# A new order of all steps, and fourteen zero products behind the first scores, in a banded-attention kernel with a gated projection

## The chip, the core and the metric

The kernel runs on one core of one Trainium2 chip. The time is the device time of one execution in microseconds (us); the median of several runs counts. A core has five engines that run side by side and wait for each other by semaphores: TensorE (PE, matrix products; PEld is its weight load), VectorE (DVE), ScalarE (ACT), GpSimd (POOL) and SyncE (SP, which here issues every transfer).

## What is computed

Eight batches of eight heads. 512 local tokens each see 32 global keys and the local keys within 32 positions; 32 global tokens see all 544 keys. The result, 8 times 544 rows of 512 numbers, goes through a gate of two products and two more products. All of it is float32.

```python
s_g = scale * q_g @ k_all.T;  out_g = softmax(s_g) @ v_all
s_l = concat(scale * q_l @ k_g.T, where(|i - j| <= 32, scale * q_l @ k_l.T, -1e9))
out_l = softmax(s_l) @ concat(v_g, v_l)
x = concat(out_g, out_l)            # 4352 rows of 512
h = ((x @ w1) * (x @ w2)) @ w3      # inner width 1024
return h @ w_out
```

## The kernel before

**Steps.** The work is cut into some 3700 steps, and each step is a small function that issues a few instructions. The names below are the tiles that the profile shows.

- `scores1` (L500) and `scores` (L515) write the scores `s` of a head or of a pair of heads. They are float32 products on 64 rows of the array, eight a pair. `minus_max` (L524, DVE) masks them, `exps` (L528, ACT) makes the exponentials in `P`.
- `transposes` (L556, L558) turn `P` on TensorE into `t` for the first 16 heads; later heads go through a transfer to memory and back (`own`). `values` (L653, L659) makes `av` from the turned weights in `PT` and `G`, `values_sum` adds the halves.
- `g_scores` (L701, L709) writes the scores `sg` of the global queries, `g_minus_max` (L728, DVE), `g_exps` (L735, ACT), `g_normalize` (L739 to L741, DVE), `g_transposes` (L747, L748, tile `tg`).
- `fold` (L944) multiplies w3 by w_out once, 64 products into the tiles `w`, from weights that come as 64-bit words and are put together by DVE and ACT (`unpack`, L864 to L868).
- `first` (L810 to L812) is the gate's product of one m and one half a or b: 12 products of 128x128 by 128x256 into `ap` or `bp`, three for each pair of heads since every operand is split in a high and a low part. There are 3264 such products. `gate_a`, `gate_b`, `gate_hi`, `gate_lo` turn a pair of results into the operands `gh` and `gl`.
- `second` (L842 to L844) is the last product, six of 128x128 by 128x512 into `acc`, 137 steps.

**What sets the order.** `list_schedule` places the steps on five engines: at each moment the engine that is free takes, of the steps whose inputs are there by the planner's own costs, the one with the smallest number in the table `DUE`. Every engine executes its instructions in the order in which they were placed, and so does SP with its transfers. After each placed step the kernel calls `idle_products` with what `IDLE` lists for that step: products on a tile of zeros that nobody reads. The planner doesn't know of these. Before, `IDLE` has seven products ahead of everything and two behind the first `sg`.

**What stands where.** The first 118 us hold `fold`, the first heads and the first global scores. Then `first` and `second` of one batch run beside the attention of the next; the last pair scores (`s31`) start at 693 us, and from about 735 us only `first` and `second` are left.

Of the kernel before, what the change touches and what calls it, by code (L numbers as in the profile page):

```python
# [30 lines left out]
def i(ap):  # L31
# [18 lines left out]
IDLE = {None: ((0, 128, 256), (0, 128, 256), (0, 128, 256), (0, 64, 256), (64, 128, 256), (0, 64, 256), (64, 128, 256),), ("sg", 0): ((0, 128, 256), (0, 128, 256),)}  # L50
# [258 lines left out]
def band_attention_glu_kernel(  # L309
# [1103 lines left out]
    with tc.manual_schedule(engines=None):  # L1413
        idle_products(IDLE[None])
        for _, n, e in list_schedule(steps, after, held):
# [6 lines left out]
            fn(*args)  # L1422
            idle_products(IDLE.get(k, ()))

# [60 lines left out]
```

## Time and profile before

| | |
|---|---|
| median of 3 runs | 841.6 us (841.11 to 842.97) |
| the profiled execution | 839.91 us |
| its span, first to last instruction | 838.1 us |
| busy: PE, DVE, ACT, POOL | 821.3, 525.6, 480.5, 327.4 us |
| granted TensorE clock, mean | 0.995 of 2.4 GHz |

The span is cut by the profiler's records; 1.8 us of the execution lie outside it. A matrix product starts while the one ahead of it still drains, so an engine that the page calls busy may run at different paces: the time from one start to the next is the pace, and the duration in a row is longer than that.

### The profile page before, as it was taken

To read this page: it belongs to the slowest core of one execution; us is meant where nothing else is said; L and a number is where in the kernel's file an instruction comes from. 1 tells how busy PE (TensorE), PEld (TensorE's weight loads), DVE (VectorE), ACT (ScalarE), POOL (GpSimd) and SP (SyncE) were. 2 spreads that over 40 slices of the span, in tenths; PEclk is the share of its full clock that TensorE was granted. 3 is DMA by queue.
4 is the path that set the end of the run, shared out by engine and by line. 5 is a ranking of instruction groups with operands and counts; after the bars stand their busy time and mean duration, and the time that the engine had idled before them with its cause. 6 is when DMAs were issued, how large, how long until landed. Compare 5 with 4: busy or idle time off the path is not lost.

```text
span 838.1 us, 17284 instructions
## 1 busy us (share of the span) xinstructions
PE 821.3 (98%) x5666; PEld 728.7 (87%) x5666; DVE 525.6 (63%) x1436; ACT 480.5 (57%) x1354; POOL 327.4 (39%) x429
## 2 busy tenths in 40 slices
PE   5999999999999999999999999999999999999998
PEld 4656679899999988998988999998999999999997
DVE  4767776756666756667767778876778755522111
ACT  3665767756666656566756576666665554422112
POOL 1112453623456554544534654554555433300000
PEclk8999999999999999999999999999999999999999
DMA  8786655434666667566666666766565544200000
GB/s 282 235 266 218 193 142 172 138 89 130 180 162 174 169 157 178 149 176 174 174 165 185 171 179 162 172 166 180 152 175 152 144 106 135 51 27 14 13 26 26
DMA packets 209842, 124.87 MB, mean 149 GB/s; under 512 B 138328, under 2 KB 171480, under 8 KB 209752
## 3 DMA queue, kind: packets, MB, share of 16 engines
q1 hardware_dynamic: 209752, 123.76, 54.0%
q8 instruction: 45, 0.74, 0.4%
q14 instruction: 45, 0.37, 0.2%
HBM read 89.52 MB, written 31.82 MB: 145 GB/s over the span
## 4 chain that ended last, share of the span: by engine, by line
PE 88%; DMA 4%; SPq 3%; DVE 2%; issue 1%; ACT 1%; POOL 0%; ACTq 0%; DVEq 0%; POOLq 0%
PE bp L810 7%; PE ap L810 7%; PE acc L842 7%; PE av L659 7%; PE bp L811 7%; PE bp L812 7%; PE acc L844 7%; PE ap L811 7%; PE acc L843 7%; PE ap L812 7%; PE w L944 7%; PE s L515 5%; PE av L653 3%; PE s L500 1%; DMA G<-gd 1%
## 5 line engine op out<-in xcount | busy, mean ns | idle before, releaser
L810 PE MATMUL ap<-x,w12h 128*128 128x256 f32 x544 | 154.0, 283 | 0.5 <-ACT as__4769 L816 0.5
L810 PE MATMUL bp<-x,w12h 128*128 128x256 f32 x544 | 153.8, 283 | 0.0
L811 PE MATMUL ap<-x,w12h 128*128 128x256 f32 x544 | 151.7, 279 | 0.0
L812 PE MATMUL ap<-x,w12l 128*128 128x256 f32 x544 | 151.7, 279 | 0.0
L811 PE MATMUL bp<-x,w12h 128*128 128x256 f32 x544 | 151.7, 279 | 0.0
L812 PE MATMUL bp<-x,w12l 128*128 128x256 f32 x544 | 151.6, 279 | 0.0
L528 ACT ACTIVATE P<-P,small 128x192 f32<-128x192 f32 (+1 forms) x256 | 121.1, 474 | 15.6 <-DVE small L524 14.9
L810 PEld LDWEIGHTS ap<-x,w12h 128*128 128x128 f32 x544 | 102.4, 188 | 4.8 <-issue 2.0
L810 PEld LDWEIGHTS bp<-x,w12h 128*128 128x128 f32 x544 | 102.3, 188 | 3.6 <-issue 1.6
L811 PEld LDWEIGHTS ap<-x,w12h 128*128 128x128 f32 x544 | 102.3, 188 | 1.5 <-issue 0.2
L811 PEld LDWEIGHTS bp<-x,w12h 128*128 128x128 f32 x544 | 102.3, 188 | 1.3
L812 PEld LDWEIGHTS bp<-x,w12l 128*128 128x128 f32 x544 | 102.9, 189 | 0.0
L812 PEld LDWEIGHTS ap<-x,w12l 128*128 128x128 f32 x544 | 102.9, 189 | 0.0
L524 DVE CUSTOM_DVE_ANT_0 P<-s,cs 128x256 f32<-128x256 f32 (+1 forms) x256 | 85.0, 385 | 4.2 <-PE s L515 2.7
L673 DVE TENSOR_TENSOR u<-av,cb 64x352 f32<-64x352 f32 x96 | 49.2, 520 | 46.3 <-ACT cb L441 45.1
L441 ACT COPY cb<-av 64x352 f32<-64x352 f32 x77 | 34.4, 447 | 59.0 <-PE av L659 51.7
L444 POOL TENSOR_TENSOR PT<-own,PT 128x512 fp32r<-128x512 f32 x36 | 48.1, 1337 | 32.1 <-ACT PT L441 23.1
L944 PE MATMUL w<-wo,w3f 128*128 128x512 f32 x128 | 59.7, 598 | 0.5 <-DVE w3f L868 0.5
L659 PE MATMUL av<-PT,vs 128*128 128x192 f32 (+3 forms) x384 | 52.8, 264 | 0.4 <-DMA PT<-TT 0.4
L515 PE MATMUL s<-kq,qp 64*128 64x192 f32 (+1 forms) x448 | 50.0, 362 | 0.0
L528 ACT ACTIVATION_READ_ACCUMULATOR P<-P,small 128x1 f32 x256 | 48.1, 188 | 0.0
L515 PEld LDWEIGHTS s<-kq,qp 64*128 64x128 f32 x448 | 39.2, 186 | 8.8 <-issue 2.2
(804 smaller groups left out, 1883.9 us busy)
## 6 DMA issues: line engine op xcount, KB each, us to landing
raw_w<-in_w_t_dram SPq DMA_DIRECT2D x24, 512.0 KB, 4.7
od<-tw SPq DMA_DIRECT2D x48, 256.0 KB, 2.5
own<-od SPq DMA_DIRECT2D x192, 64.0 KB, 2.5
kq<-in_kd_t_dram SPq DMA_DIRECT2D x32, 304.0 KB, 3.4
kpr<-in_kp_t_dram SPq DMA_DIRECT2D x32, 272.0 KB, 3.8
out_dram<-o_None SPq DMA_DIRECT2D x33, 256.0 KB, 2.8
qp<-in_q_t_dram SPq DMA_DIRECT2D x32, 256.0 KB, 3.4
R<-rd SPq DMA_DIRECT2D x64, 128.0 KB, 3.5
```

Of the source, the lines that this page charges most:

```text
L515: nc.tensor.matmul(st[:, x, c : c + w], q[r, 128 * e : 128 * e + 128], k[r, o : o + w], start=(e % 2 == 0), stop=True, skip_group_check=True)
L524: nc.vector.tensor_tensor_reduce(blk(n, e), s, masks[e], -0.125, 3.0e38, ALU.add, ALU.min, T["mn", n][:, e : e + 1])
L528: nc.scalar.activation(blk(n, e), blk(n, e), AF.Exp, bias=T["mn", n][:, e : e + 1], scale=-1.0, accum_out=T["sm", n // 2][:, n % 2, e : e ...
L659: nc.tensor.matmul(av[0:r, o : o + 32 * (s1 - s0)], v[:, 0:r], PT[:, s0:s1, y, j], start=False, stop=(j % 2 == 1 and (plain or y == 1)), s ...
L673: nc.vector.tensor_add(T["u", n // 2][r : r + 64, x], T.pop(("av", n, x))[r : r + 64, 0:352], T["cb", n][r : r + 64, x])
L810: nc.tensor.matmul(d, wh[:, k, c, :], x[:, 0, 0:w], start=(k == m % 2 == 0), stop=False, skip_group_check=True)
L811: nc.tensor.matmul(d, wh[:, k, c, :], x[:, 1, 0:w], start=False, stop=False, skip_group_check=True)
L812: nc.tensor.matmul(d, wl[:, k, c, :], x[:, 0, 0:w], start=False, stop=(k == 3), skip_group_check=True)
L842: nc.tensor.matmul(a, gh[:, m % 2, sl], wh[:, c], start=(m == 0), stop=False, **part)
L843: nc.tensor.matmul(a, gh[:, m % 2, sl], wl[:, c], start=False, stop=False, **part)
L844: nc.tensor.matmul(a, gl[:, m % 2, sl], wh[:, c], start=False, stop=(m in (5, 7)), **part)
L944: nc.tensor.matmul(T["w34", t], T["w3f", t, j // 4][:, j % 4], T["wo"][:, j], start=(j == 0), stop=(j == 7))
```

## The change

`DUE`, the table of one number a step, is replaced, and `IDLE` gets an entry: fourteen products on zeros behind step `("s", 0)`, the scores of head 0.

```diff
-IDLE = {None: (...), ("sg", 0): ((0, 128, 256), (0, 128, 256),)}
+IDLE = {None: (...), ("s", 0): ((0, 128, 256),) * 14, ("sg", 0): ((0, 128, 256), (0, 128, 256),)}
...
 DUE = tuple(int(x) / 100 for x in """
-    127000 102500 146000 347000 352500 321500 661500 103500 94000 191000 74500 1861000 161000 220000 490000 1831500 243500 18500 668000 298500 323500 996500 35000 491500
...
```

The matrix products are the same ones, 5233 before and 5247 after with the fourteen. Which step follows which on TensorE is different. Counted over the program, of the pair scores `s` 18 stood behind a step of `first` and 9 behind one of `second`; now it is 4 and 23. Of the values `av` of heads 16 to 63, 39 stood behind `first` and 15 behind `second`; now 14 and 34. Of the later global scores `sg`, 11 stood behind `first` and 7 behind `second`; now 23 and 1; 4 had a `second` behind them, now none. `first` and `second` follow each other 135 times before and 141 times after.

**Place 1, the start, TensorE.** Here are its first steps, before and after. `idle` are the zero products.

```order
L500 MATMUL s_142<-kq_114,qp_116 128x192
L500 MATMUL s_142<-kq_114,qp_116 128x256 x2
L500 MATMUL s_142<-kq_114,qp_116 128x192
L701 MATMUL sg_176<-kpr_137,QG_112 128x272 x2
L388 MATMUL idle_102<-vgs 128x256 x2
L701 MATMUL sg_191<-kpr_128,QG_112 128x272 x2
L944 MATMUL w_0_197<-wo,w3f_0_165 128x512
L556 MATMUL t_205<-cs,P_79 128x128 x4
L558 MATMUL t_205<-cs,P_79 128x128 x3
L944 MATMUL w_1_219<-wo,w3f_0_213 128x512
L747 MATMUL tg_228<-cs,Pg_187 128x128 x4
L748 MATMUL tg_228<-cs,Pg_187 128x128
```

```order
L500 MATMUL s_150<-kq_121,qp_116 128x192
L500 MATMUL s_150<-kq_121,qp_116 128x256 x2
L500 MATMUL s_150<-kq_121,qp_116 128x192
L388 MATMUL idle_102<-vgs 128x256 x14
L701 MATMUL sg_177<-kpr_114,QG_112 128x272 x2
L388 MATMUL idle_102<-vgs 128x256 x2
L701 MATMUL sg_192<-kpr_133,QG_112 128x272 x2
L556 MATMUL t_205<-cs,P_79 128x128 x4
L558 MATMUL t_205<-cs,P_79 128x128 x3
L747 MATMUL tg_226<-cs,Pg_189 128x128 x4
L748 MATMUL tg_226<-cs,Pg_189 128x128
L944 MATMUL w_0_241<-wo,w3f_0_214 128x512
```

Fourteen products came between `s` and the first `sg`. Two products `w` stood ahead of `tg`, on either side of `t`; now the first `w` stands behind `tg`. Both lists go on with the scores of the next head (`s1` in the text) and its values. Further on, the turned weights of head 1 (the second `t`) had scores and a `w` behind them and now have the values `av` of the same head behind them at once.

**Place 1, the start, VectorE.** The masks of head 0 (L524), the global scores (L728) and the weights (L864, L868), before and after.

```order
L524 ISA P_79,small<-s_142,cs 128x192
L524 ISA small 128x1
L524 ISA P_79,small<-s_142,cs 128x256
L524 ISA small 128x1
L524 ISA P_79,small<-s_142,cs 128x256
L524 ISA small 128x1
L524 ISA P_79,small<-s_142,cs 128x192
L524 ISA small 128x1
L864 TENSOR_SCALAR raw_w12s_1_135<-raw_w12s_1_135 128x256
L868 SCALAR_TENSOR_TENSOR raw_w12s_1_135<-raw_w12s_1_135 128x256
L728 ISA Pg_187,small<-sg_176,cs 64x544
L728 ISA small 64x1
```

```order
L524 ISA P_79,small<-s_150,cs 128x192
L524 ISA small 128x1
L864 TENSOR_SCALAR raw_w12s_1_129<-raw_w12s_1_129 128x256
L868 SCALAR_TENSOR_TENSOR raw_w12s_1_129<-raw_w12s_1_129 128x256
L728 ISA Pg_189,small<-sg_177,cs 64x544
L728 ISA small 64x1
L524 ISA P_79,small<-s_150,cs 128x256
L524 ISA small 128x1
L524 ISA P_79,small<-s_150,cs 128x256
L524 ISA small 128x1
L524 ISA P_79,small<-s_150,cs 128x192
L524 ISA small 128x1
```

Before, all four masks of head 0 stood ahead of the first L728; now three of the four stand behind it. Beyond these rows, the first merged `wo` (L868) stood ahead of the second L728 and now stands behind L741. On SP the first transfers were `kq`, `qp`, a block of weights, `QG`; they are now `kpr`, `qp`, `cs`, `kq`, a block of weights, `QG`, so that the scores of head 0, which need `kq` and `qp`, wait for the fourth transfer and no longer for the second, while the mask `cs` went from ninth to third and the `kpr` of the first `sg` from eleventh to first.

**Place 2, the last pair scores, TensorE.** The steps around `s31`, of before and after.

```order
L810 MATMUL bp6_0_6_8939<-x6_3_0_8376,w12h7_1059 128x256
L811 MATMUL bp6_0_6_8939<-x6_3_0_8376,w12h7_1059 128x256
L812 MATMUL bp6_0_6_8939<-x6_3_0_8376,w12l7_1060 128x256
L515 MATMUL s31_0_9049<-kq31_8421,qp31_8401 128x192 x2
L515 MATMUL s31_0_9049<-kq31_8421,qp31_8401 128x256 x2
L515 MATMUL s31_1_9054<-kq31_8421,qp31_8401 128x256 x2
L515 MATMUL s31_1_9054<-kq31_8421,qp31_8401 128x192 x2
L810 MATMUL bp6_1_0_9075<-x6_0_1_7460,w12h0_88 128x256
L811 MATMUL bp6_1_0_9075<-x6_0_1_7460,w12h0_88 128x256
```

```order
L842 MATMUL acc6_0_128_8700<-w34h5_882,gh__8969 128x512
L843 MATMUL acc6_0_128_8700<-w34l5_883,gh__8969 128x512
L844 MATMUL acc6_0_128_8700<-w34h5_882,gl__8994 128x512
L515 MATMUL s31_0_9055<-kq31_8448,qp31_8374 128x192 x2
L515 MATMUL s31_0_9055<-kq31_8448,qp31_8374 128x256 x2
L515 MATMUL s31_1_9060<-kq31_8448,qp31_8374 128x256 x2
L515 MATMUL s31_1_9060<-kq31_8448,qp31_8374 128x192 x2
L810 MATMUL ap6_1_0_8999<-x6_0_1_7478,w12h1_90 128x256
L811 MATMUL ap6_1_0_8999<-x6_0_1_7478,w12h1_90 128x256
```

`s31` stood between two steps of `first`; now a step of `second` stands ahead of it.

## Rows read from the trace of the kernel before

**Rows 1.** The page, busy time by engine: us, share of the span, instructions.

```profile
PE 821.3 (98%) x5666; PEld 728.7 (87%) x5666; DVE 525.6 (63%) x1436; ACT 480.5 (57%) x1354; POOL 327.4 (39%) x429
```

**Rows 2.** Timeline of PE: start us, duration us, engine, line, tiles, shape, count, idle.

```profile
255.27 0.28 PE L810 MATMUL ap<-x,w12h 128*128 128x256 f32 x1
...
259.91 0.28 PE L812 MATMUL ap<-x,w12l 128*128 128x256 f32 x1
...
738.74 0.28 PE L810 MATMUL ap<-x,w12h 128*128 128x256 f32 x1
...
744.27 0.28 PE L812 MATMUL ap<-x,w12l 128*128 128x256 f32 x1
```

**Rows 3.** Groups of PE by line in 255.2:260.2, 215:692, 695:832: count, busy us, mean ns.

```profile
L812 PE MATMUL bp<-x,w12l 128*128 128x256 f32 x8 | 2.2, 276 | 0.0
...
L812 PE MATMUL ap<-x,w12l 128*128 128x256 f32 x368 | 102.3, 278 | 0.0
...
L812 PE MATMUL bp<-x,w12l 128*128 128x256 f32 x128 | 36.0, 281 | 0.0
```

**Rows 4.** Timeline of PE around s31 and s11.

```profile
691.82 0.28 PE L810 MATMUL bp<-x,w12h 128*128 128x256 f32 x1
...
693.07 0.28 PE L812 MATMUL bp<-x,w12l 128*128 128x256 f32 x1
693.27 1.78 PE L515 MATMUL s<-kq,qp 64*128 64x192 f32 x16
694.99 0.38 PE L810 MATMUL bp<-x,w12h 128*128 128x256 f32 x1
...
249.99 1.78 PE L515 MATMUL s<-kq,qp 64*128 64x192 f32 x16
251.70 0.38 PE L810 MATMUL ap<-x,w12h 128*128 128x256 f32 x1
```

**Rows 5.** Timeline of PE in the first 31 us.

```profile
5.17 1.67 PE L500 MATMUL s<-kq,qp 64*128 64x192 f32 x8
13.56 2.15 PE L701 MATMUL sg<-kpr,QG 128*128 128x272 f32 x4 [6.72 <-issue]
15.51 1.91 PE L388 MATMUL idle<-vgs 128*128 128x256 f32 x4
17.21 1.50 PE L701 MATMUL sg<-kpr,QG 128*128 128x272 f32 x4
18.55 1.02 PE L944 MATMUL w<-wo,w3f 128*128 128x512 f32 x2
...
22.55 1.78 PE L500 MATMUL s<-kq,qp 64*128 64x192 f32 x8
...
30.76 0.49 PE L558 MATMUL t<-cs,P 128*128 128x128 f32 x3
```

**Rows 6.** Busy us of PE, PEld, DVE, ACT, POOL (count), PEclk, DMA share, GB/s.

```profile
16.00:17.00 1.00, 1.00 (x4) 0.82 (x3) 0.90 (x4) 0.69 (x1) 0.00 (x0) 0.50 1.21 250
```

**Rows 7.** Timeline of ACT and DVE in the first 33 us.

```profile
5.46 0.44 ACT L866 ACTIVATE raw_w12s<-raw_w12s 128x256 f32<-128x256 f32 x1 [3.45 <-DMA raw_w12s<-in_w_t_dram]
...
11.40 0.36 DVE L524 CUSTOM_DVE_ANT_0 P<-s,cs 128x192 f32<-128x192 f32 x1
...
15.75 0.72 DVE L728 CUSTOM_DVE_ANT_1 Pg<-sg,cs 64x544 f32<-64x544 f32 x1 [1.64 <-PE sg L701]
...
19.51 0.75 ACT L735 ACTIVATE Pg<-Pg,small 128x544 f32<-128x544 f32 x1 [2.67 <-DVE small L728]
...
20.05 0.69 DVE L868 SCALAR_TENSOR_TENSOR w3f<-raw_w 128x512 int32<-128x512 int32 x1
...
21.24 0.50 DVE L741 TENSOR_SCALAR Pg<-Pg,small 128x544 f32<-128x544 f32 x1
...
32.37 0.69 DVE L441 COPY PT<-t 128x512 f32<-128x512 f32 x1 [1.79 <-ACT G L441]
```

**Rows 8.** Waits of PE: waited for, us in total, times, longest us.

```profile
PE av L653 <- DMA G<-gd: 3.3, 5, 1.3
```

More of the change, by code (lines that the diff above doesn't have):

```diff
@@ L47 @@
 )
-IDLE = {None: ((0, 128, 256), (0, 128, 256), (0, 128, 256), (0, 64, 256), (64, 128, 256), (0, 64, 256), (64, 128, 256),), ("sg", 0): ((0, 128, 256), (0, 128, 256),)}
+IDLE = {None: ((0, 128, 256), (0, 128, 256), (0, 128, 256), (0, 64, 256), (64, 128, 256), (0, 64, 256), (64, 128, 256),), ("s", 0): ((0, 128, 256),) * 14, ("sg", 0): ((0, 128, 256), (0, 128, 256),)}
 MARGIN, LATE, MAIN = 0, 0.0, 1e9
```

311 rows, old and new, of the table DUE are left out of this document.

## The prediction, made before the changed kernel ran

> **What bounds the kernel now.** I read the page first. TensorE is busy for 98% of the span [rows 1], and among its waits only one kind comes to more than a microsecond in the body of the program: `av` on the transfer of `G`, 3.3 us in five waits [rows 8]. The rest of its idle time lies in the first 31 us. An order can therefore gain in two ways: fewer gaps, or the same products at a closer pace. Since a busy TensorE may run at different paces, I then took the timeline and divided the time between two starts by the number of products. From 255.27 to 259.91 there are 41 steps in 4.64 us, 113.2 ns each; from 738.74 to 744.27 there are 47 in 5.53 us, 117.7 ns [rows 2]. It is the same instruction, 128x128 by 128x256, with no wait in either stretch. The duration in a group's row tells the two apart: the mean is 276 ns where all are fast and 281 where all are slow [rows 3]. So a mean says how many were slow: 278 in 215 to 692 is two fifths (278-276 over 281-276), and 281 in 695 to 832 is all of them. With 12 products in each of 272 steps there are 3264, of which about 2150 lie in the middle stretch and 744 in the last. Slow are .4 x 2150 = 860 and 744, and at 4.5 ns each (117.7-113.2) they cost 3.9 and 3.3 us.
>
> What changes the pace is seen at the scores. At 691.82 to 693.07 there are 11 steps in 1.25 us, 113.6 ns each: fast. Then `s31` comes between two steps of `first` [rows 4], and behind it everything to the end is slow [rows 3]. From 195 us on seven pair scores met a fast `first` and had `first` behind them; all seven left the slow pace (first at 231, last at 693). Behind a `second` eight were measurable, and all eight left the fast one; 249.99 is one [rows 4]. A global score behind `first` with `second` behind it turned fast into slow three times of three. The values `av` mostly leave the pace as it was (changed in 2 of 23). That is a correlation in one trace, without a cause that I can show.
>
> The start is bound otherwise. TensorE ends `s` at 6.84 and has nothing until `sg` at 13.56 [rows 5]; while it idles the granted clock falls to .5 of 2.4 GHz, the level of 1.2, where it stands from 11.2 to 18 us [rows 6]. Two zero products (four records) take 1.70 us there, from 15.51 to 17.21 [rows 5].
>
> **The change part by part: the order behind the start.** No product is added or taken away behind the start, so the sum of durations at one pace is the same. Pair scores behind `second` go from 9 to 23, those behind `first` from 18 to 4, and none of the global scores has a `second` behind it any more. If I walk the new order with the successions above, the fast pace is kept for most of the middle, about 12% slow in place of 40%, since what remains are the four `s` behind `first` and the doubtful `av`: 2150 x .28 x 4.5 = 2.7 us. The last `s31` now stands behind `second`, so the tail starts fast; `first` and `second` alone kept the pace there before. Taking a tenth as slow, it gains 744 x .9 x 4.5 = 3.0 us. Together 5.7; I take **-5.5**. The bounds are 0, if the succession is not the cause, and -7.2, if all of both stretches is fast.
>
> The Trainium skill, page "TensorE: Matmul & The Clock Gate", section "Wait — 56ns, not 53.3ns?", speaks against this gain: it gives one pace for back-to-back products at 2.4 GHz, the columns over the clock and about 2.5 ns more, 109 ns for 256 columns. By it an order couldn't change the pace, and the term would be 0. The trace doesn't agree: it has two paces, 113 and 118 ns, and no run here shows 109.
>
> Waits: TensorE's other waits in the body add to some 7.6 us with the 3.3 of [rows 8]. In the new order the distance from each `s` to its masks, from `av` to its transfer and from `first` to the gate is about as long, counted in products between; some are shorter, as the values directly behind `t` of head 1, which the start includes. I take 0, with 2.5 either way (a third of the waits).
>
> **The start.** I walk it with the durations of the rows. `s` needed the second transfer and now needs the fourth. The third had landed by 5.46, when ACT was released by it [rows 7]; by count the fourth is there at 5.46 x 4/3 = 7.3 at most, 5.5 at least, and I take 6.7, nearer the later end because `kpr` and `cs` are large tiles. `s` takes 1.7 [rows 5]: 8.4. The zero products at the full clock are half of 1.70 for two, .43 each; fourteen take 6.0, to 14.4. They fill the gap, so the clock should stay up: the first `sg` took 1.95 from start to start, the two products 1.70, part of the second `sg` was slow too, and half of that (some 2.3 us) is no longer lost. `sg` at full clock is 1.0 to 1.1, to 15.5. VectorE's mask of it (L728) starts .24 behind and takes .72 [rows 7]: 16.4. In front of the second `sg` there now stand three masks of head 0, at .36 [rows 7] and somewhat more: 17.4. The order shows that this `sg` waits for VectorE. It ends at 18.5, its L728 at 19.3. From the start of ACT's L735, 19.51, to the end of L741, 21.74, are 2.23 [rows 7]; so L741 ends at 21.6. `tg` and the merge of the first `wo`, moved behind L741 (.3 and .69 as in the L868 of 20.05 [rows 7]) come to 22.6, one `w` at .86 to 23.5. So `s1` starts at 23.5 in place of 22.55 [rows 5], .95 late, with one `w` fewer done, .86. Then `av` of head 1 stands directly behind its `t`: before, `t` ended at 31.25 [rows 5] and its copies at 33.06 [rows 7], with `s` and `w` in between to hide that; now some 1.5 of the 1.8 us are open. The sum is .95 + .86 + 1.5 = **+3.3**. The bounds are -2.3, the clock alone with everything else covered, and +6.0, the fourth transfer at 7.3 with the merges of `wo` and the copies each later by their own length. What hides the fourteen products is the wait for the transfers that ended at 13.56; since `kpr` now comes first, that cover may be gone, and then they cost TensorE itself their six us less the clock, which is in the walk.
>
> **Sum.** 839.91 - 5.5 + 3.3 + 0 = 837.7 for the profiled execution. The median lies 1.7 above that execution, so 837.7 + 1.7 = **839.4** against 841.6.
>
> **The rivals.**
> 1. *The start costs nothing, the pace comes.* If the walk's waits are hidden (s0 is there at 5.5, copies are fast), the start gives 0 to -2.3: 841.6 - 5.5 = 836.1 down to 833.8. For it: the clock loss is in the rows. Against it: three masks and the merge really moved in front of `sg` and `w`.
> 2. *The pace doesn't come, the start costs.* This is the slower side. The pace of a stretch would be set by something other than what stands ahead of `s`, for instance by the phase in which the products meet VectorE's and ACT's reads, and the new order would be slow about as often: 841.6 + 3.3 = 844.9. It is slower than before by over 1.7 us when the slow share of the middle and the tail together, now 1604 of 2894 or 55%, stays above 43%: the gain is then under 2894 x .12 x 4.5 = 1.6 of the start's 3.3. By the page's rule named above the order couldn't move the pace either, and the sum is this one. For it: 7 of 7 and 8 of 8 are one trace; against it: the split is clean.
> 3. *The clock falls all the same.* After the fourteen, TensorE waits for masks (16.6 to 17.4) and for `tg` (18.5 to 21.6). If the granted clock falls to .5 in there as at 11.2, then up to six us of products run at half pace, 2 to 3 us more: 839.4 + 2.5 = 841.9.
> 4. *Nothing of it moves the time*: the paces keep their shares and the start loses what the clock gains: 841.6.
>
> **How the numbers follow.** The forecast 839.4 (837 to 842, the waits' 2.5 either way) has 45%; rival 1 18%, rival 2 17%, rival 3 10%, rival 4 10%. A measurement can tell about 0.2%, 1.7 us, from no change: faster is below 839.9, slower above 843.3. The forecast lies half a microsecond below that bound, so of its 45% I give 27 to faster and 18 to same; rival 1 is faster, rival 2 slower but for 1, rivals 3 and 4 together same with 13, faster with 3, slower with 4. That gives faster .48, same .32, slower .20. The range for 8 in 10 reaches from rival 1's middle, 834.5, to rival 2's 845.0. Both signs hold chances; the likeliest case alone is 837 to 842.
>
> **What would show it.** Pace: the means of L812 go from 278 to about 277 in the middle and from 281 to 276 or 277 in the tail, and `s31` has 113 ns behind it as ahead of it. If the tail is at 281, the succession isn't the cause. Start: granted clock 1.0 from the first `s` to the second, `s1` near 23.5, an idle of 1.5 ahead of the `av` behind the second `t`. If `s1` is at 22 or below, rival 1 holds; a clock of .5 between 18 and 22 is rival 3. Waits: `av` on the transfer of `G` between 1 and 6 us in all; above that, the new order has shortened a distance that I took as equal.

## The result and the profile after

The changed kernel took 851.76 us in the median of six runs (847.19 to 853.75), the kernel before 841.49 (841.11 to 843.04): a ratio of 1.0099 with a 95% interval of 1.0080 to 1.0118. It is slower, outside the range of the prediction, and on the side that had a chance of 0.20. Two of the six runs are at 847.2 and four between 851 and 854; the trace is of a short one, 847.22 us with a span of 845.4, 7.3 more than before. On another chip, beside the experiments, it took 847.12 against 838.79, 8.3 us more. The experiments are read against the runs of before on their own chip.

The page's busy time and the groups of L812 (engine, tiles, count, busy us, mean ns), in 215:692 and 695:832, answer to [rows 1] and [rows 3]:

```profile
PE 825.8 (98%) x5694; PEld 727.3 (86%) x5694; DVE 530.5 (63%) x1435; ACT 478.0 (57%) x1352; POOL 326.9 (39%) x432
```

```profile
L812 PE MATMUL ap<-x,w12l 128*128 128x256 f32 x360 | 100.4, 279 | 0.0
L812 PE MATMUL bp<-x,w12l 128*128 128x256 f32 x350 | 97.1, 278 | 0.0
...
L812 PE MATMUL ap<-x,w12l 128*128 128x256 f32 x128 | 35.4, 277 | 0.0
L812 PE MATMUL bp<-x,w12l 128*128 128x256 f32 x127 | 35.2, 277 | 0.0
```

The tail is fast now, 277 in place of 281. The timeline of TensorE around `s31` shows it as [rows 4] does for before (start us, duration us, line, tiles, count):

```profile
700.83 0.40 PE L844 MATMUL acc<-w34h,gl__8994 128*128 128x512 f32 x1
701.16 1.78 PE L515 MATMUL s<-kq,qp 64*128 64x192 f32 x16
...
704.36 0.28 PE L810 MATMUL bp<-x,w12h 128*128 128x256 f32 x1
...
705.60 0.28 PE L812 MATMUL bp<-x,w12l 128*128 128x256 f32 x1
```

From 704.36 to 705.60 are 11 steps in 1.24 us, 113 ns each, behind `s31`. In the middle the mean did not fall; the stretch at half clock shown below holds it up, and without that stretch, in `after_no_zeros`, it is 277. The start, to be read beside [rows 5], and the granted clock there, beside [rows 6] (the third number from the end is the clock):

```profile
1.19 4.29 PE L388 MATMUL idle<-vgs 128*128 128x256 f32 x14 [1.19 <-DVE vgs L385]
6.94 2.20 PE L500 MATMUL s<-kq,qp 64*128 64x192 f32 x8 [1.46 <-DMA kq<-in_kd_t_dram]
9.07 7.50 PE L388 MATMUL idle<-vgs 128*128 128x256 f32 x28
16.40 1.08 PE L701 MATMUL sg<-kpr,QG 128*128 128x272 f32 x4
...
22.73 0.63 PE L747 MATMUL tg<-cs,Pg 128*128 128x128 f32 x4 [1.87 <-DVE Pg L741]
...
24.50 1.78 PE L500 MATMUL s<-kq,qp 64*128 64x192 f32 x8
...
32.53 0.75 PE L653 MATMUL av<-G,PT 128*128 128x288 f32 x2 [2.11 <-ACT G L441]
```

```profile
8.00:11.00 3.00, 3.00 (x9) 2.11 (x8) 1.43 (x5) 1.08 (x4) 0.00 (x0) 0.52 0.94 293
11.00:14.00 3.00, 3.00 (x14) 2.63 (x13) 0.00 (x0) 0.00 (x0) 0.00 (x0) 0.92 1.10 345
```

The zeros stand from 9.07 to 16.40, 7.3 us, with the clock at half until a little past 11 us, and `s1` starts at 24.50. The first step of `first` starts at 125.0 us, at 118.8 before.

TensorE's waits (waited for: us in total, times, longest), which answer to [rows 8], and the clock behind the longest one of the middle:

```profile
PE av L653 <- DMA G<-gd: 5.8, 5, 1.8
...
PE bp L810 <- DVE g__5252 L820: 1.2, 1, 1.2
```

```profile
450.73 0.37 PE L653 MATMUL av<-G,vgs 128*128 128x288 f32 x1 [1.83 <-DMA G<-gd]
```

```profile
452.00:454.00 2.00, 2.00 (x11) 2.00 (x11) 0.63 (x2) 1.74 (x6) 0.35 (x2) 0.50 0.71 179
```

Behind 1.83 us of waiting the clock falls to .5, and 15 products of `first` take 217 ns each: another 1.6 us. So the change did what it says, the tail got the pace that was forecast, and yet more was lost elsewhere. To see where, I priced each step of TensorE at the lowest tenth of the times that its kind took from start to start in the traces of before, after and fourteen of the experiments below, took zeros as nothing, and subtracted the sum from the time elapsed. What is left is the time lost in gaps, slow paces and zeros, by stretch:

```
us lost                 to 118  118-215  215-480  480-700  700-end   sum
before                    19.3      5.4     12.6      5.8      3.1  46.2
before_s31                19.5      5.7     10.7      5.3      0.7  41.9
after                     25.3      4.5     17.4      4.8      1.5  53.5
after_no_zeros            20.5      3.8     17.0      4.5      1.2  47.0
before_no_g               19.3      5.8      7.7      7.2      3.1  43.1
after_no_zeros_no_g       21.9      4.0      8.3      5.1      1.4  40.7
```

The first and the third row differ by 7.3, the difference of the spans: 6.0 of it at the start, 4.8 between 215 and 480 us, and 3.5 gained in the rest. The split is good to a microsecond or two: each row is one execution, `before_s31` stands 4.3 below `before` where their spans differ by 4.9, and it lost 1.9 less between 215 and 480 us although nothing was changed there.

### The profile page after: what moved, and what is told of

Same layout as the page of the kernel before. It is cut to its first block, busy times and chain, and to the rows that moved or that the text cites. A ratio compares the mean times of both kernels' runs of the same rounds, so it can differ in the third digit from the quotient of the medians.

```text
span 845.4 us, 17383 instructions
## 1 busy us (share of the span) xinstructions
PE 825.8 (98%) x5694; PEld 727.3 (86%) x5694; DVE 530.5 (63%) x1435; ACT 478.0 (57%) x1352; POOL 326.9 (39%) x432
## 4 chain that ended last, share of the span: by engine, by line
PE 83%; DMA 5%; SPq 4%; DVE 2%; ACT 2%; issue 2%; POOL 1%; ACTq 0%; POOLq 0%; DVEq 0%
PE av L659 7%; PE ap L810 7%; PE w L944 7%; PE acc L844 6%; PE acc L842 6%; PE ap L811 6%; PE ap L812 6%; PE acc L843 6%; PE bp L810 6%; PE bp L811 6%; PE bp L812 6%; PE s L515 4%; PE av L653 3%; PE s L500 2%; DMA G<-gd 2%
## 5 line engine op out<-in xcount | busy, mean ns | idle before, releaser
L812 PE MATMUL ap<-x,w12l 128*128 128x256 f32 x544 | 151.4, 278 | 0.0
L812 PE MATMUL bp<-x,w12l 128*128 128x256 f32 x544 | 150.9, 277 | 0.0
L812 PEld LDWEIGHTS ap<-x,w12l 128*128 128x128 f32 x544 | 102.9, 189 | 0.0
L812 PEld LDWEIGHTS bp<-x,w12l 128*128 128x128 f32 x544 | 102.5, 188 | 0.0
L524 DVE CUSTOM_DVE_ANT_0 P<-s,cs 128x256 f32<-128x256 f32 (+1 forms) x256 | 85.3, 384 | 7.5 <-PE s L500 3.6
L444 POOL TENSOR_TENSOR PT<-TGr,PT 128x128 fp32r<-128x128 f32 x38 | 18.4, 485 | 87.3 <-ACT PT L441 66.9
```

What stands on the lines that cost most here:

```text
L524: nc.vector.tensor_tensor_reduce(blk(n, e), s, masks[e], -0.125, 3.0e38, ALU.add, ALU.min, T["mn", n][:, e : e + 1])
L812: nc.tensor.matmul(d, wl[:, k, c, :], x[:, 0, 0:w], start=False, stop=(k == 3), skip_group_check=True)
```

## The experiments

**The same kernel again: `after_again`.**

> The changed kernel once more, unchanged, to see what its times of 847.2 (two of six) and 851.5 to 853.7 (four of six) consist of. If the extra 4.6 us come from the granted clock falling to .5 behind waits of TensorE (as behind the wait of 1.83 us at 448.9 us in the trace of after, where it stood at .5 for some 3 us), a trace of a longer execution shows more such stretches, each worth 1.5 to 2.3 us, at the waits of the start or of av on G. If they come from the pace of the products, its mean of L812 between 695 and 832 us goes back from 277 to 281 ns. If from the transfers, the waits of av on G are longer in sum than the 5.8 us seen.

Measured: 847.12 us (840.95 to 849.90), ratio 1.0087 (1.0057 to 1.0117). The profiled execution, 849.21, has its first step of `first` at 128.2, 3.2 later than the shorter execution of the first trace, and the middle and the tail as there. At its start the clock stays at .5 for longer, and falls once more behind the wait for `tg`:

```profile
11.00:14.00 3.00, 3.00 (x9) 2.37 (x8) 0.09 (x1) 0.00 (x0) 0.00 (x0) 0.50 1.04 334
...
26.00:29.00 3.00, 3.00 (x8) 1.46 (x7) 2.20 (x5) 1.14 (x4) 0.00 (x0) 0.65 0.67 193
```

The zeros took 8.4 us here. The first theory holds for these two traces: between one execution and the next the clock at the start makes some 3 us. In the middle each of the two traces has one fall of the clock, at 452 and 455 us. A still longer execution, 855.61 us, was traced in `after_s31`; it has its fall at 280 us instead. What makes the rest of the spread of 9 us was not seen.

**The zeros alone: `after_no_zeros` and `before_zeros`.** One entry of `IDLE` is taken out of the new order, or put into the old one:

```diff
-IDLE = {None: (...), ("s", 0): ((0, 128, 256),) * 14, ("sg", 0): ((0, 128, 256), (0, 128, 256),)}
+IDLE = {None: (...), ("sg", 0): ((0, 128, 256), (0, 128, 256),)}
```

> The new order without the fourteen zero products (the old IDLE table). Theory 1: in the new order nothing keeps the first sg waiting behind s, so the zeros are in the path: they stood from 9.07 to 16.40 us; without them the first sg starts at 9 to 10 us, at half the clock until about 13, s1 at some 19 in place of 24.50, and the time falls by 4 to 6 us, to about 842 for the short executions. Theory 2: the start is bound by the loads of weights and masks, which run on beside the zeros; then the first step of first still starts near 125 us and the time falls by less than 1.5 us. Theory 3: the clock that the zeros keep up is worth more than their length; then the time rises by 1 to 3 us.

> The old order with the fourteen zero products behind the first s. There the first sg waited until 13.56 us for its eleventh transfer, 6.72 us. Theory 1: the zeros fit into that gap (6.84 to 12.8 us at full clock, to 14.2 if they run at half the clock at first as in the trace of after, where they took 7.33 us); the granted clock then stays up from 11 to 18 us and the time falls by 1 to 2.3 us, to about 839.5 to 840.5. Theory 2: what the products gain is lost in waits on masks and exponentials behind them; the time stays within 0.7 us of 841.5.

Measured: the new order without zeros 843.05 us, ratio 1.0051 (1.0037 to 1.0065), so by the medians the zeros cost 4.1 us there, by the ratios 3.0, and the two intervals overlap a little; the traces are clearer. Nothing kept the first `sg` waiting once they were gone:

```profile
7.07 3.32 PE L500 MATMUL s<-kq,qp 64*128 64x192 f32 x8 [0.94 <-DMA kq<-in_kd_t_dram]
10.32 2.18 PE L701 MATMUL sg<-kpr,QG 128*128 128x272 f32 x4
...
19.51 1.78 PE L500 MATMUL s<-kq,qp 64*128 64x192 f32 x8
```

`s1` starts at 19.51 and `first` at 120.0, 5 us earlier. Theory 1 holds. The old order with the zeros took 837.48, ratio 0.9990 (0.9970 to 1.0009): its trace has the clock at 1.00 through the start, the zeros run from 7.45 to 13.76 and `sg` starts at 14.11, `first` at 117.2, 1.6 earlier than in the old trace. The median agrees in size (1.3), but the interval takes in no change: not settled.

```profile
5.84 1.67 PE L500 MATMUL s<-kq,qp 64*128 64x192 f32 x8
7.45 6.31 PE L388 MATMUL idle<-vgs 128*128 128x256 f32 x28
```

**The pace: `before_s31` and `after_s31`.** One step is moved on TensorE, by name, behind the planner: in the old order a step of `second` to directly ahead of `s31` (there `sp`, 31), in the new one a step of `first` (there with the longer code of the next experiment, which does the same).

```diff
+MOVED = ((('second', 12, 5, None), ('sp', 31)),)      # after_s31: (('first', 13, 1, 0), ('sp', 31))
...
-        for _, n, e in list_schedule(steps, after, held):
+        order = list_schedule(steps, after, held)
+        for a, b in MOVED:
+            name = [steps[n][0] for _, n, _ in order]
+            x = order.pop(name.index(a))
+            name.remove(a)
+            order.insert(name.index(b), x)
+        for _, n, e in order:
```

> The old order with one step moved on TensorE: the step of second that stood three steps of first ahead of the last pair scores s31 now stands directly ahead of them. Nothing else is moved. Theory 1 (what stands ahead of the scores sets the pace behind them): the last 744 products of first run at 113 and no longer at 118 ns, the mean of L812 between 695 and 832 us falls from 281 to 276 or 277, and the time falls by 3.0 to 3.3 us, to about 838.3. Theory 2 (the succession only went along with something else, such as the time at which the products meet the other engines): the mean stays at 281 and the time within 0.7 us of 841.5.

> The changed kernel with one step moved on TensorE: a step of first that stood directly behind the last pair scores s31 now stands ahead of them, so that s31 stands between two steps of first as in the kernel before. Theory 1 (what stands ahead sets the pace): the tail goes back to 118 ns, the mean of L812 between 705 and 830 us from 277 to 281, and the time rises by 3.0 to 3.3 us over the changed kernel, to a ratio of 1.0125. Theory 2: any move near s31 may turn the pace by chance; then the tail may stay at 277 and the ratio at 1.0087.

Measured: `before_s31` 835.43, ratio 0.9960 (0.9945 to 0.9976), 3.4 us less; `after_s31` 848.93, ratio 1.0117 (1.0085 to 1.0149), 1.8 us over `after_again`, which ran on another chip; the ratios are 0.0030 apart, 2.5 us. The groups of the gate's product in 705:830, first of `before_s31` (where the line is L815, three lines further down), then of `after_s31`:

```profile
L815 PE MATMUL bp<-x,w12l 128*128 128x256 f32 x114 | 31.5, 277 | 0.0
```

```profile
L812 PE MATMUL bp<-x,w12l 128*128 128x256 f32 x108 | 30.4, 281 | 0.0
```

Both ways one step decides the pace of all that follows. In the time lost from 700 us on, `after_s31` has 4.6 and the changed kernel 1.5, the 3.1 that were expected; the times alone, with intervals that overlap, would not show it. In the trace of `before_s31` the tail makes 2.4 of the 4.3 us that were won; the rest lies ahead of the move and is the difference between two executions.

**The pace in the middle: `before_scores`.** `MOVED` has seven pair scores and three global ones; a step takes along those that need it or that it needs (`out` and `store`, for instance).

```diff
+MOVED = (
+    (('second', 1, 7, None), ('sp', 10)), (('second', 4, 7, None), ('sp', 16)), (('second', 6, 7, None), ('sp', 20)),
...
+    (('first', 2, 4, 1), ('second', 2, 0, None)), (('first', 3, 0, 1), ('second', 2, 5, None)),
...
+)
```

> The old order with all seven pair scores that had turned the fast pace into the slow one put directly behind a step of second (s10, s16, s20, s21, s22, s27, s31; out and store move with the second where they depend on it), and at three global scores (sg11, sg12, sg29) the step of first that came second now ahead of the step of second. Theory 1 (what stands ahead of the scores sets the pace): nearly all steps of first from 215 us on run at 113 ns, the mean of L812 falls to 277 in the middle and in the tail, and the time falls by 5 to 6 us, 3.4 of it what s31 alone gave: ratio 0.993 to 0.994. Theory 2 (only the tail can be turned): ratio 0.996, as with s31 alone, and the middle stays at 278.

Measured: 837.62, ratio 0.9978 (0.9961 to 0.9994), no better than `s31` alone. L812 is 277 in the tail and 278 in 215:692, and the middle lost 12.3 us, like before. The numbers are those of theory 2, but its reason is not: the changed kernel turned the middle. Counted by step between 215 and 703 us, 68 of 204 were slow before, 57 of 204 here and 27 of 195 in the changed kernel: the moves turned few of the steps, since the pace fell into the slow one in other ways, behind `av` and `sg` above all, and what was won is not in the time. At the pair scores themselves the succession holds. I went through all 18 traces of this document from 195 us on (several have the same order again) and took every group of pair scores that has `first` directly behind it. Where a `second` stood ahead, that `first` was fast 267 times of 272; where a fast `first` stood ahead, it was slow 64 times of 64.

**The waits: `after_no_zeros_av` and `after_no_zeros_sp`.** The first moves steps of TensorE (`first` of m 0 for batch 2, for instance) ahead of the values that waited, the second moves transfers on SP:

```diff
+    (('first', 2, 0, 1), ('av', 17, 0)), (('first', 3, 1, 0), ('av', 21, 0)), ...      # _av
+    (('mi', 17), ('me', 17)), (('mi', 21), ('invo', 11)), ...                          # _sp
```

> The new order without the zeros, and with one or two steps of first (one of second too) moved from behind the values av of heads 17, 21, 25, 35, 37 and 39 to ahead of them: there TensorE waited for the transfer of G or PT, in the trace without the zeros some 1.9, 1.2, 2.3, 1.3, 3.3 and 1.0 us from the start of the step ahead to av, and at head 37 the granted clock fell behind the wait. Theory 1: the 4.3 us by which the order without zeros was slower than the kernel before are these waits and the clock behind them; the moved steps fill them, the waits of av on G fall from 6.0 to under 2 us, the stretch from 215 to 480 us gets 5 us shorter, and the time falls from 1.005 of the kernel before to 0.999 or below. Theory 2: the transfer of G is issued behind the end of the values of the head before, and SP, ACT or POOL move on with TensorE's delay; the waits stay or turn up at the gate, and the time stays within 0.002 of 1.005. Theory 3: what is lost lies in the start; the same numbers as theory 2, but with the waits gone.

> The new order without the zeros, TensorE's order untouched; only on SP the transfer of G from memory (L602) for the heads 17, 21, 25, 35, 37 and 39 is issued ahead of what stood between it and the values of the head before (the edges into PT, L591 and L592, and for some heads the loads of k and v or the sums). Theory 1 (SP's order makes TensorE wait for G): the waits of av on G fall from 6.0 to under 3 us and the time by 2 to 4 us, ratio 1.000 to 1.003. Theory 2 (the edges are wanted just as soon): the waits move to PT and the ratio stays within 0.0015 of 1.005.

Measured: 843.80, ratio 1.0050 (1.0033 to 1.0067), and 843.46, ratio 1.0066 (1.0039 to 1.0093): neither gained. The waits in 118:830, of `after_no_zeros`, of `_av` and of `_sp`:

```profile
PE av L653 <- DMA G<-gd: 6.0, 4, 3.0
```

```profile
PE bp L810 <- DVE g__3561 L820: 1.7, 1, 1.7
PE ap L810 <- ACT as__5768 L816: 1.6, 1, 1.6
PE av L653 <- DMA G<-gd: 1.3, 2, 0.9
PE bp L810 <- DVE g__2299 L820: 1.3, 1, 1.3
```

```profile
PE av L659 <- DMA PT<-TT: 2.3, 3, 1.1
PE acc L844 <- DVE gl__5186 L444: 1.8, 1, 1.8
```

The waits on `G` fell from 6.0 to 1.3 and 0.9 us, and others came up at the gate, or at the edges in `PT`: theory 2 in both, with `_sp` at the edge of its bound (1.0066 for 1.0065). The clock is not it either. The expectation has it fall at head 37, but that was the trace with the zeros; without them the products behind that wait, the longest of all, ran at full pace:

```profile
445.39 0.37 PE L653 MATMUL av<-G,vgs 128*128 128x288 f32 x1 [2.99 <-DMA G<-gd]
...
446.66 0.28 PE L811 MATMUL ap<-x,w12h 128*128 128x256 f32 x1
```

So these waits look like the places where a chain through other engines shows; filling one moved it.

**Less work for TensorE: `before_less` and `after_no_zeros_less`.** In `second`, for odd m of the batches 1 to 3, the product with `w34l` is left out:

```diff
-            nc.tensor.matmul(a, gh[:, m % 2, sl], wl[:, c], start=False, stop=False, **part)
+            if m % 2 == 0 or key[0] not in (1, 2, 3): nc.tensor.matmul(a, gh[:, m % 2, sl], wl[:, c], ...)
```

> The kernel before with less work for TensorE between some 240 and 490 us: in second, for the batches 1 to 3 and odd m, the product of gh with the low part of w3*w_out (L843) is left out, 6 x 4 x 2 products of 229 ns, 11.0 us. If TensorE sets the time of this stretch, the time falls by 9 to 11 us; if the transfers and the other engines set part of it, by less, since TensorE then waits for what it no longer covers. For the order of before, where TensorE waited for some 4 us in this stretch, both theories expect 7 to 10 us: ratio 0.988 to 0.992.

> The same products left out (L843 for batches 1 to 3 and odd m, 11.0 us) in the new order without the zeros, whose ratio with all products was 1.005. Theory 1 (in the new order a loop through SP, the transfers, VectorE and GpSimd sets the pace between 215 and 480 us, so that waits filled at one place turn up at another): the time falls by much less than before's, by 6 us or less, ratio 0.998 or above. Theory 2 (TensorE sets the time there too, and its waits are single accidents of the order): it falls by as much as before's, ratio 0.993 to 0.997.

Measured: 835.06, ratio 0.9947 (0.9928 to 0.9967), and 838.50, ratio 0.9993 (0.9970 to 1.0016): 4.4 us less than before (2.8 to 6.0 by the interval), where 7 to 10 were expected, and 4.9 less than 1.0051, which was measured on another chip. Of 11.0 us taken from TensorE four to five came back as time, in both orders. Executions differ: the one traced in `before_less` is the shortest of nine and has a span 8.1 us shorter than before. Theory 1 falls as I had put it, since the old order is no different; so does theory 2, that TensorE sets the time. In the new order the waits of `av` on `G` rose to 10.1 us:

```profile
PE av L653 <- DMA G<-gd: 10.1, 6, 2.8
```

Behind three of them, of 2.09, 2.51 and 2.84 us, the granted clock fell to .5, which the trace of `after_no_zeros` doesn't have:

```profile
224.00:227.40 3.40, 3.40 (x18) 3.40 (x17) 2.47 (x5) 2.55 (x7) 3.21 (x7) 0.50 0.19 54
...
445.80:449.20 3.40, 3.40 (x18) 3.40 (x18) 1.77 (x4) 2.74 (x8) 1.75 (x5) 0.51 0.84 203
```

The products of `first` in them start every 213 ns in place of 113, so these falls cost some 1.5 us each: in this execution a good part of what did not come back is the clock behind longer waits.

**The loop through memory: four kernels.** The edge weights of a head go from `TT` to memory (`gd`) and back into `G`, and from `TT` into `PT`, all issued by SP; a head's may land only when the values of the head before are done. The longest wait of the middle in the changed kernel shows the way of one head, on SP:

```profile
440.47 1.09 SPq L597 DMA_DIRECT2D gd<-TT  x2
...
444.15 0.64 SPq L591 DMA_DIRECT2D PT<-TT  x1
...
446.15 0.99 SPq L602 DMA_DIRECT2D G<-gd  x2
```

The second part of `gd` landed at 444.11 and the values of the head before were done by then, but SP was busy with other transfers until 446.15; `G` landed at 450.59, and `av` started at 450.73. These transfers are left out for heads 18 to 41:

```diff
             k = steps[n][0]
+            if k[0] in ('mo', 'mi') and 17 < k[1] < 42:      # _pt: ('mo', 'mi', 'me')
+                continue
```

> The kernel before, with the way of the edge weights through memory left out for heads 18 to 41 (some 237 to 490 us): the transfers of TT to gd (L597) and of gd to G (L602), 96 issues on SP; G keeps older numbers, all else is computed. Theory 1 (this way, SP's issues and the landing, is the loop that takes back what TensorE gains in the middle): TensorE's waits on G are gone, 3.3 us in the whole trace, and SP is freer; the time falls by 2 to 4 us, ratio 0.995 to 0.998. Theory 2 (the edges into PT or the gate take its place at once): ratio 0.998 or above.

> The new order without the zeros, with the same transfers (L597, L602, heads 18 to 41) left out. Theory 1 (in the new order this loop closes later, and that is its loss in the middle): the waits on G, 6.0 us, and the fall of the clock at head 37 go, and the time falls by 4 to 6 us to the time of before_no_g or below, ratio 0.998 to 1.000 from 1.005. Theory 2 (another loop takes over, as when the values were moved or SP's order was changed): ratio 1.003 or above.

> As before_no_g, and the transfers of the edges from TT into PT (L591, L592) left out too for heads 18 to 41. Theory 1: no more than before_no_g, within 0.001. Theory 2: now the waits are gone, ratio 0.995 to 0.998. If the gate's chain through ACT and VectorE bounds the stretch, neither brings more than 0.002.

> The new order without the zeros, the transfers into G and those of the edges into PT both left out for heads 18 to 41. Theory 1: as after_no_zeros_no_g, within 0.001. Theory 2, in the form that G and the edges come one behind the other on SP and only both together are the loop: ratio 0.997 to 1.000. Theory 3 (the loss lies with the gate's chain, L816 to L820, and the masks on ACT and VectorE): ratio 1.003 or above, with waits on these.

Measured, with the kernels above for comparison:

```
                               old order                   new order, no zeros
all work                       1                           1.0051 (1.0037 to 1.0065)
without gd and G               0.9961 (0.9946 to 0.9976)   0.9922 (0.9897 to 0.9947)
without the edges in PT too    0.9946 (0.9932 to 0.9960)   0.9920 (0.9904 to 0.9936)
```

The row of all work in the new order was measured on another chip than the four kernels. The old order gains 3.3 us, the new one 10.8, nearly twice what its waits on `G` came to, and more than the 4 to 6 that were expected; that the edges in `PT` bring anything more is not shown, since the intervals overlap. TensorE's waits on `G` in 118:830, 6.0 us with all transfers, are down to 1.4 in the new order:

```profile
PE av L653 <- DMA G<-gd: 1.4, 1, 1.4
```

The time lost in 215 to 480 falls from 12.6 to 7.7 and from 17.0 to 8.3, so that the 4.4 between the orders there shrink to 0.6. Theory 1 holds in this: the new order's loss in the middle goes with these transfers, which cost it 7.5 us more than the old order by the medians (some 5 to 10 by the intervals) and 3.8 by these traces. With them gone the new order is 3.3 us faster than the old one, the two intervals all but apart. That comes near what the tail's pace is worth in `before_s31`, but the traces do not put it there alone: they differ by 2.4, of which the tail makes 1.7, the stretch from 480 to 700 us 2.1 and that from 118 to 215 us 1.8, while the start loses 2.6 and the middle 0.6.

Two things stay open. Which moves of the new order make the transfers dearer was not found; SP's order of six transfers is not it. And a rival was not tested: leaving them out also takes 96 issues off SP, which issues everything in order. Added up from its rows, SP is issuing for 204 of the 265 us from 215 to 480 in the kernel before (77%), and for 156 without `gd` and `G`. Whether it is this one way through memory or SP's full queue as a whole, the runs do not say. SP's share alone doesn't make the loss: from 480 to 700 us it is 73% in the old order and 74% in the new one, and less time is lost there.

**A version that beats both: `before_best` and `before_s31_best`.** The old order, the zeros, `s31`, and a step of `first` ahead of the values of heads 25, 27 and 37; `before_best` has the other scores of `before_scores` too.

```diff
+MOVED = (
+    (('second', 12, 5, None), ('sp', 31)), (('first', 4, 0, 1), ('av', 25, 0)),
+    (('first', 4, 5, 1), ('av', 27, 0)), (('first', 7, 0, 1), ('av', 37, 0)),
+)
...
+IDLE = {None: (...), ("s", 0): ((0, 128, 256),) * 14, ("sg", 0): ((0, 128, 256), (0, 128, 256),)}
```

> The moves of before_scores, the fourteen zero products behind the first s in the old order, and one step of first moved ahead of the values av of heads 25, 27 and 37, where TensorE waited for G. Sum of the parts: 5 to 6 us of pace, 1 to 1.8 of the start, 2 of waits: 8 to 9 us, ratio 0.990. If the parts are in each other's way (the start's gain waited away later, since the loads don't come earlier), the ratio is that of before_scores within 0.001.

> The old order with only those changes that had a place of their own: s31 behind a step of second, the fourteen zeros behind the first s, and one step of first ahead of the values of heads 25, 27 and 37. If the six other moves of scores in before_best bring nothing, as the runs of before_s31 (0.996) and before_scores (0.998) suggest, the ratio is that of before_best, 0.9941, or lower: 0.992 to 0.994. If they bring their two to three us of pace, it is 0.996.

Measured: 834.24, ratio 0.9941 (0.9924 to 0.9957), and 833.37, ratio 0.9920 (0.9894 to 0.9946), 5.2 and 5.7 us less than before. Both beat both kernels; between them the intervals overlap. The first falls short of the 8 to 9 us of its sum, the second lies where it was expected. Their intervals overlap with that of `before_s31` (0.9945 to 0.9976) too, the second's by a hair, so what the zeros and the three moved steps add to `s31` is not shown.

## Why the prediction was wrong

- **What bounds the kernel: wrong, and the root of it.** "TensorE is busy for 98%" was taken to mean that a microsecond of TensorE is a microsecond of time. At 11.0 us less work it was two fifths of one between 240 and 490 us (a quarter to a half by the interval). A busy share of 98% and a way through other engines that is just hidden look alike in the page; only a change of the load told them apart.
- **The waits, 0 with 2.5 either way: the step that failed.** Distances counted in products on TensorE said nothing of SP's queue and of the way through memory. Between 215 and 480 us the trace lost 4.8 us more than before, and the loss went when the transfers through `gd` and `G` were left out, which cost the new order 7.5 us more than the old one by the medians and 3.8 by the traces. The sign that I had named, the waits on `G` between 1 and 6 us, would not have told: they stood at 5.8, and the rest of the loss showed at the gate, at `PT` and in the clock. The 7.6 us of waits in the body, from which I took the bounds, were too many as well: [rows 8] and the smaller waits beside it add to 5.4.
- **The pace, -5.5: the mechanism right, the size smaller.** The succession sets the pace at the scores, by single moves in both directions, and rival 2 falls. `before_s31` gained 3.4 for the 3.0 of the tail; in the changed kernel the tail went from 118 to 114.5 ns on the average, 2.5 us at 744 products, and the time lost there fell by 1.6. In the middle the slow steps fell from 33% to 14% (the walk said 40 to 12), which at 2150 products and 4.5 ns is 1.8 us; as time none of it is seen, since TensorE alone doesn't set it there. `before_scores` shows that the scores don't decide every turn. One reading of mine was off: the values `av` alone changed the pace at four places of the trace of before (237, 310, 432 and 498 us), not at two. The one pace that the Trainium skill gives (page "TensorE: Matmul & The Clock Gate", section "Wait — 56ns, not 53.3ns?") would have made the term 0; the same runs don't agree with it, with 113 and 118 ns behind one moved step.
- **The start, +3.3: the sign right, the size too small.** The first step of `first` came 6.2 us late in the trace. My walk had `s` at the full clock (1.7; it took 2.1) and the zeros at 6.0 (7.3), since it took the clock to stay up. But `s` waited 1.46 us for its fourth transfer, and the clock fell ahead of the zeros. Behind `t` of head 1 there were 2.1 us open and not 1.5. And "what hides the fourteen products" was gone, as I wrote: `sg` could start at 10.3. I compared the walk with before's 13.56 and not with that, so I didn't see that the zeros alone are worth 3 to 4 us of time, 5 in the traces.
- **The sum.** In the trace the start lost 6.0 (+3.3 was forecast), the stretch from 215 to 480 us lost 4.8, and the others gained 3.5 together: +7.3 where the terms came to -2.2. By the medians on the chip of the experiments the zeros make +4.1 and the order without them +4.3, together 8.3 unrounded. To split the latter into the transfers, +7.5, and a remainder of -3.3 is a subtraction; that it adds up proves nothing, and the remainder holds more than the pace of the tail. On the first chip 10.3 were measured, and the 2.0 are open.
- **Rival 3, a second fall of the clock**, was in the trace of `after_again` and, at 452 us, in the first. I had given it 10% and only the start.

## What to carry to other kernels

Before the gain of an order is summed up from one engine's rows, take some microseconds of work from that engine in the stretch and see what comes back: an engine at 98% need not set the time. Zero products meant to keep the clock up can pay only in a gap that stays (whether they paid here, in the old order, is not settled); in a new order price them against the earliest start of what stands behind them. A wait that is filled and turns up elsewhere hints that the chain lies outside the engine that waits; look for it by leaving out one of its links, and ask what else that link used.

## What was not expected of the hardware

- Which step stands ahead of one group of 64-row products decides whether the 128x128 by 128x256 products of the next 130 us start every 113 or every 118 ns; the cause is not known.
- The zeros did not hold the clock where TensorE had been idle for 1.46 us just before `s` (.52 from 8 to 11 us), and did where `s` followed at once (1.00 in `before_zeros`).
- The length of a wait alone did not tell whether the clock falls: behind 1.83 us it fell (`after`, at 452 us), behind 2.99 us it did not (`after_no_zeros`, at 445 us), at the same head.
- In `after_no_zeros` the clock column shows 1.00 from 8 to 14 us, yet `sg` took 1.97 us from start to start (10.32 to 12.29), as at a clock of .5 in the kernel before (1.95), and `s` 3.25, twice the 1.61 of `before_zeros`. The trace has no record of the clock before 13.7 us, and the column says 1.00 where nothing was recorded:

```profile
8.00:11.00 3.00, 3.00 (x9) 2.08 (x8) 1.01 (x5) 0.61 (x2) 0.00 (x0) 1.00 0.96 318
11.00:14.00 3.00, 3.00 (x9) 2.35 (x8) 1.89 (x8) 0.73 (x3) 0.00 (x0) 1.00 1.09 334
```

```profile
12.29 1.71 PE L388 MATMUL idle<-vgs 128*128 128x256 f32 x4
```

Where the record of the clock is missing, the pace of the products tells it.
